# Talking-heads attention before two MLPs: pairs of tiles taken two at a time, or singly

## The chip, the cores and the metric

The kernel runs on one core of a Trainium2 chip. The metric is the time of one execution on the device in microseconds; where several executions were timed it is their median.

Words used below: TensorE does the matmuls, VectorE (DVE in the profile), ScalarE (ACT) and GpSimd (POOL) the elementwise work, and SyncE (SP) issues most DMAs. Each engine works through its own instructions in order and waits for the others by semaphores. A matmul writes into a bank of PSUM, of which there are eight, and another engine copies the result out. In the profile PE is TensorE's matmuls and PEld its weight loads.

## What is computed

Four batches, 12 heads, 448 positions, head dimension 64, all in f32. The heads are mixed before and after the softmax:

```
scores = scale * q @ k^T                       # per head
scores = einsum('bhij,hg->bgij', scores, w_pre)
attn   = softmax(scores, axis=-1)
attn   = einsum('bhij,hg->bgij', attn, w_post)
x      = attn @ v                              # then reshaped to (1792, 768)
x      = square(relu(x @ w_in)) @ w_out        # first MLP, 768 -> 2048 -> 768
h      = x @ w2_in
out    = (h * clip(h + 3, 0, 6) / 6) @ w2_out  # second MLP
```

## The kernel before

**Stages.** The batches are taken in two groups of two. Each group has an attention stage (class `Attention`, line 150) and then an MLP stage (`Mlps` for the first group, line 627; `Blocks` for the second, line 896). The program is one list of instructions in an order written out by hand: every engine gets its instructions in the order in which the Python code calls them.

**Tiles and pairs.** The 448 rows of a batch are cut into tiles of 10 query rows, with all 12 heads side by side on the partitions. Eleven or twelve tiles are a chunk; a group has eight chunks, 90 tiles, and 45 pairs of tiles. A pair is the unit of the work, and *slot* m is the turn of pair m's postmix.

**What happens to a chunk and a pair.**

- `score` (206) is a *visit*: the products of q and k for two heads of one chunk, into two banks. ScalarE copies the one bank (line 209), VectorE the other (211), into the chunk's scores `s`. A chunk takes six visits.
- `fetch` (221) has SP issue two DMAs (230) that bring a pair's rows of `s` into tiles `t`, so that heads lie on the partitions. It is called five slots ahead (`FETCH`).
- `premix` (234): TensorE mixes the heads (242), into two banks.
- `top` (245): VectorE takes each row's maximum (257). `soft` (259): ScalarE takes the exponential and its sum (266). `invert` (270): VectorE adds 1e-9 and inverts (274, 275). `scale` (278): GpSimd multiplies the postmix weights by the inverse, into `w2s` (286).
- `postmix` (290): TensorE mixes the heads again, with the result transposed (299); it is 32 f32 products, which the trace shows as 64 matmuls, each with its own weight load. `keep` (304): ScalarE (318) and VectorE (320) copy its two banks into the chunk's `a`.
- `values` (323): once a chunk's `a` is complete, TensorE multiplies it by V (333; the trace shows 96 matmuls), and VectorE copies the result into `xr` (343).

**Banks.** The pool `ps` (111) has four tags of two banks each. Premixes take `by` and `bm` in turn. Visits, products with V and postmixes take `bs` and `bo`, alternately where the tag comes from `in_turn` (202). A user of a bank waits until the copies of the bank's last user are done.

**The order.** `plan` (388) sets which visits, products with V and loads fall into which slot. `run` (556) goes through the slots. Most of them go in rounds of two, by `two_slots` (493). TensorE's order in a round of slots m and m+1 is: premix m+2, a visit "V", premix m+3, a visit "W", a finished chunk's products with V if there are any, postmix m, postmix m+1, a visit "C". Around these the other engines get, in order: exponentials of m+1 (if still to do) ahead of the first premix; maxima of m+2 on both sides of visit V; exponentials of m+2 behind the second premix; maxima of m+3; exponentials of m+3 ahead of the products with V, or ahead of postmix m+1; inverse and scale of m+2 and copies of m behind postmix m; the same of m+3 and m+1 behind postmix m+1. `rounds` (428) and `places` (432) say where a visit goes. The first slot of the first group and the first three of the second (`PAIRED`, 26) are single, by `slot` (446), and there all visits use the tag `bs`. The slots of negative m, ahead of the first postmix, go through `slot` as well.

**Beside the slots.** In the second group `beside` (1027) is called once for every slot, after the round: it has SP load and store, and GpSimd compute (617), sums of weights for the last MLP stage. `early` (657) converts the first MLP's first unit, called ahead of some products with V. After the last slot `closing` (581) does the last chunk's products with V, into a bank of `bm` and one of `by`.

## Time and profile before

| | |
|---|---|
| Median of 3 runs | 1267.08 us (1262.11 to 1267.51) |
| The profiled execution's own time | 1264.64 us |
| Its span, first to last instruction | 1262.8 us |
| Mean granted clock of TensorE | 0.992 |
| Busy: TensorE / VectorE / ScalarE / GpSimd | 1212.4 / 912.1 / 655.6 / 259.5 us |

The profile is of one execution; its times count from the first instruction. The first attention stage runs from some 16 to 199 us, the first group's MLPs to 667, the second attention stage to 857, and the last MLPs to the end. "Busy" of TensorE is from start to end of its matmuls, which overlap one another, so the time that a group of matmuls takes is read from the starts of two groups that follow each other. In a row of the timeline the bracket at the end tells how long the engine sat idle before the row and what ended it; "issue" stands where nothing that the profile shows was waited for. [...]

### The profile page before, as it was taken

To read this page: it belongs to the slowest core of one execution; us is meant where nothing else is said; L and a number is where in the kernel's file an instruction comes from. 1 tells how busy PE (TensorE), PEld (TensorE's weight loads), DVE (VectorE), ACT (ScalarE), POOL (GpSimd) and SP (SyncE) were. 2 spreads that over 40 slices of the span, in tenths; PEclk is the share of its full clock that TensorE was granted. 3 is DMA by queue.
4 is the path that set the end of the run, shared out by engine and by line. 5 is a ranking of instruction groups with operands and counts; after the bars stand their busy time and mean duration, and the time that the engine had idled before them with its cause. 6 is when DMAs were issued, how large, how long until landed. Compare 5 with 4: busy or idle time off the path is not lost.

```text
span 1262.8 us, 32217 instructions
## 1 busy us (share of the span) xinstructions
PE 1212.4 (96%) x13108; PEld 1058.1 (84%) x13108; DVE 912.1 (72%) x1561; ACT 655.6 (52%) x1268; POOL 259.5 (21%) x349
## 2 busy tenths in 40 slices
PE   8889989999999999999998898979999999999998
PEld 4666778999999999998886666768999999999998
DVE  5666877777665688775556576766977996899885
ACT  5555664545232355532326465657678555456642
POOL 2111133444000033310101343450001220001422
PEclk9999999999999999999999999989999999999999
DMA  6635445766976667677774787757976766685442
GB/s 208 201 118 187 143 147 147 229 190 207 297 220 211 187 203 224 195 235 234 246 267 163 215 271 233 245 198 246 297 247 208 253 200 217 204 285 174 136 135 91
DMA packets 131636, 262.44 MB, mean 208 GB/s; under 512 B 13728, under 2 KB 100384, under 8 KB 131488
## 3 DMA queue, kind: packets, MB, share of 16 engines
q1 hardware_dynamic: 128032, 254.87, 63.2%
q10 hardware_dynamic: 3456, 5.51, 1.2%
q8 instruction: 103, 1.69, 0.6%
q14 instruction: 45, 0.37, 0.1%
HBM read 151.80 MB, written 69.99 MB: 176 GB/s over the span
## 4 chain that ended last, share of the span: by engine, by line
PE 89%; DMA 3%; issue 3%; ACT 3%; DVE 2%; SPq 1%; ACTq 0%; POOL 0%; DVEq 0%; POOLq 0%
PE ps_h L763 18%; PE ps_a L780 18%; PE ps_y L1179 16%; PE ps_w L1079 15%; PE ps_v L333 6%; PE ps_o L299 5%; PE ps_s L199 5%; PE ps_m L242 4%; ACT p L266 2%; DMA t<-s 1%; DVE mx L257 1%; SPq L230 1%; ACT s L209 1%; DVE s L211 0%; DMA first<-in_dram 0%
## 5 line engine op out<-in xcount | busy, mean ns | idle before, releaser
L299 PEld LDWEIGHTS ps_o<-w2s,p 64*64 64x64 f32 x5760 | 102.9, 135 | 49.8 <-issue 41.2
L299 PE MATMUL ps_o<-w2s,p 64*64 64x60 f32 x5760 | 108.6, 220 | 33.0 <-issue 29.4
L780 PE MATMUL ps_a<-gh,wh 128*128 128x448 f32 x384 | 140.2, 365 | 0.0
L780 PE MATMUL ps_a<-gh,wl 128*128 128x448 f32 x384 | 138.4, 360 | 0.0
L722 DVE TENSOR_TENSOR wl<-arena,wh 128x768 fp32r<-128x768 f32 x63 | 61.8, 981 | 102.0 <-ACT wh L721 99.9
L1168 POOL TENSOR_TENSOR o<-gi,o 128x448 fp32r<-128x448 f32 x28 | 57.4, 2052 | 339.4 <-ACT o L1163 232.6
L266 ACT ACTIVATE p<-ps_m,mx 128x448 f32<-128x448 f32 x180 | 112.5, 633 | 23.3 <-DVE mx L257 20.4
L286 POOL TENSOR_SCALAR w2s<-w2f,rz 128x60 f32<-128x60 f32 x180 | 54.6, 317 | 306.2 <-DVE rz L275 215.9
L721 ACT ACTIVATE wh<-arena 128x768 fp32r<-128x768 f32 x63 | 52.8, 839 | 122.8 <-PE ps_a L780 113.8
L257 DVE TENSOR_REDUCE mx<-ps_m 128x1 f32<-128x448 f32 x180 | 104.0, 615 | 11.5 <-PE ps_m L242 10.5
L242 PE MATMUL ps_m<-t,w1f 64*64 64x448 f32 (+1 forms) x720 | 105.2, 566 | 5.1 <-DMA pr<-keep 2.2
L1179 PE MATMUL ps_y<-o,wx 128*128 128x448 f32 x504 | 105.3, 362 | 0.0
L199 PE MATMUL ps_s<-k,q 64*64 64x448 f32 x672 | 99.3, 567 | 4.0 <-ACT s L209 2.6
L1179 PEld LDWEIGHTS ps_y<-o,wx 128*128 128x128 f32 x504 | 94.5, 187 | 6.3
L1179 PE MATMUL ps_y<-o,wh 128*128 128x448 f32 x336 | 99.3, 363 | 0.0
L318 ACT ACTIVATE a<-ps_o 128x480 f32<-128x480 f32 (+1 forms) x98 | 57.2, 595 | 79.3 <-PE ps_o L299 78.5
L756 POOL TENSOR_TENSOR gl<-g,gh 128x448 fp32r<-128x448 f32 x40 | 53.3, 1333 | 203.9 <-ACT gh L755 159.9
L780 PE MATMUL ps_a<-gl,wh 128*128 128x448 f32 x240 | 87.0, 362 | 0.0
L333 PEld LDWEIGHTS ps_v<-a,v 128*64 128x64 f32 x1536 | 75.8, 140 | 12.1 <-issue 6.6
L209 ACT ACTIVATE s<-ps_s 128x448 f32<-128x448 f32 x87 | 47.3, 543 | 69.8 <-PE ps_s L199 65.1
L333 PE MATMUL ps_v<-a,v 128*64 128x110 f32 (+1 forms) x1536 | 79.2, 264 | 1.0 <-DVE a L320 0.9
L780 PEld LDWEIGHTS ps_a<-gh,wh 128*128 128x128 f32 x384 | 72.1, 188 | 9.5 <-issue 4.9
(117 smaller groups left out, 2898.6 us busy)
## 6 DMA issues: line engine op xcount, KB each, us to landing
arena<-in_dram SPq DMA_DIRECT2D x63, 768.0 KB
t<-s SPq DMA_DIRECT2D x176, 210.0 KB
keep<-arena SPq DMA_DIRECT2D x63, 384.0 KB
pr<-keep SPq DMA_DIRECT2D x88, 192.0 KB
wr<-sums_in SPq DMA_DIRECT2D x64, 192.0 KB
wr<-sums_out SPq DMA_DIRECT2D x64, 192.0 KB
low<-wl SPq DMA_DIRECT2D x28, 384.0 KB
wr<-keep SPq DMA_DIRECT2D x48, 192.0 KB
```

The source lines that it names most:

```text
L199: nc.tensor.matmul(out[e][to:to + half_p, :S], lhsT=q[own, to:to + half_p], rhs=keys[own], start=True, stop=True)
L209: nc.scalar.activation(self.s(c)[:, 2 * k, :], out[0][:, :S], AF.Copy)
L242: nc.tensor.matmul(out[a][to:to + half_p, :S], lhsT=w1f[own], rhs=t[own], start=True, stop=True)
L257: nc.vector.reduce_max(mx[:, a:a + 1], out[a][:, :S], axis=AX.X, negate=True)
L266: nc.scalar.activation(pt, o[:, :S], AF.Exp, bias=mx[:, a:a + 1], accum_out=z[:, a:a + 1])
L299: nc.tensor.matmul(out[r][to:to + KB, at:at + G * RI2], lhsT=pt[own, keys:keys + KB], rhs=w2s[own], start=True, stop=True)
L333: nc.tensor.matmul(xo[e * D:(e + 1) * D, k * n:(k + 1) * n], lhsT=self.v[:, q, g, :], rhs=self.aa[c][:, q, g, :n], start=(q == 0), stop=(q ...
L722: nc.vector.tensor_tensor(out=wl, in0=self.wr(n), in1=f(wh), op=ALU.subtract)
L763: nc.tensor.matmul(hp[:, :S], lhsT=lw[:, c * P:(c + 1) * P], rhs=rw[:, c, cols], start=(c == 0 and k == 0), stop=(c == KC - 1 and k == 2))
L780: nc.tensor.matmul(acc[d, e][:, :S], lhsT=lw[:, wc], rhs=rw[fc, e], start=(fc == 0 and k == 0), stop=(fc == NF - 1 and k == 2))
L1079: nc.tensor.matmul(to[:, :S], lhsT=lw[:, wc], rhs=rw, start=(d == 0 and j == 0), stop=(d == DB - 1 and j == 2))
L1179: nc.tensor.matmul(self.acc[d][:, :S], lhsT=lw[:, wc], rhs=rw, start=(u == 0 and q == 0 and j == 0), stop=(u == NU // 2 - 1 and q == UF - ...
```

## The change

Rounds of two slots are gone: every slot from 0 on goes through the new `slot`, which takes one pair. Its order is: fetches; exponentials of pair m+1; premix and both maxima of m+2; a visit "A"; inverse and scale of m+1; products with V if there are any; postmix m; copies of m; a visit "C"; loads of V. The six visits of a chunk are spread over the five slots of its window by the new `places`: one "C" in the first slot, one "A" in each of the others, and one more "C" in the third. All visits, postmixes and products with V in these slots take their banks from `in_turn`, and so do the closing products. The slots of negative m go through `before`, which keeps their order. In the second group's first two slots the six visits of its second chunk stand as "A", "A", "C".

```diff
--- before.py
+++ after.py
@@ -23,7 +23,6 @@
 RAW = 2
 EARLY = 3
 EARLY_AT = 23
-PAIRED = (1, 3)
 IDLE = 2
 GROUP = 2
 PAIRS = 3
@@ -161,7 +160,7 @@
             self.swap = [exchanged(tiles_of(S, NB), i) for i in range(len(self.tiles))]
             self.n = -(-len(self.tiles) // 2)
             self.live, self.ss, self.aa, self.ap, self.xr = {}, {}, {}, None, None
-            self.ks, self.n_raw, self.raw, self.at, self.late, self.turn, self.place = None, 0, None, {}, False, 1, {}
+            self.ks, self.n_raw, self.raw, self.at, self.turn, self.place = None, 0, None, {}, 1, {}
             if gi == 0:
                 self.first_opening()
             self.plan()
@@ -403,12 +402,9 @@
                     for k in range(EARLY, nk):
                         put(top - nk + 1 + k, self.score, c, k)
                     continue
-                if c == 1:
-                    when = [2 * k // nk for k in range(nk)]
-                else:
-                    places = self.places(last[c - 2] - FETCH + 1, top)[-nk:]
-                    when = [slot for slot, _ in places]
-                    self.place.update({(c, k): place for k, (_, place) in enumerate(places)})
+                places = self.places(0 if c == 1 else last[c - 2] - FETCH + 1, top, nk)
+                when = [slot for slot, _ in places]
+                self.place.update({(c, k): place for k, (_, place) in enumerate(places)})
                 for j in range(2):
                     put(when[j * KP] - 4, self.fetch_q, c, j)
                 for k in range(nk):
@@ -425,38 +421,30 @@
             for v in range(NV):
                 put(1 + 3 * v, self.fetch_v, self.batches[0], v)
 
-        def rounds(self, m):
-            m -= PAIRED[self.gi > 0]
-            return None if m < 0 else m % 2
-
-        def places(self, low, top):
-
-            out = []
-            for m in range(low, top + 1):
-                at = self.rounds(m)
-                if at is None:
-                    out += [(m, "A")] * (2 if m == low + 1 else m > low)
-                    continue
-                if at == 0 or m > low:
-                    out.append((m, "VW"[at]))
-                if at == 1:
-                    out.append((m, "C"))
-            return out
-
-        def slot(self, m):
+        def places(self, low, top, count):
+
+            if top < low:
+                return [(2 * k // count, "AAC"[k % (count // 2)]) for k in range(count)]
+            at = [(low, "C")] + [(m, "A") for m in range(low + 1, top + 1)]
+            more = [(m, "C") for m in range(low + 2, top + 1)]
+            return sorted(at + more[:count - len(at)], key=lambda x: (x[0], x[1]))
+
+        def before(self, m):
+
             work = self.at.get(m, [])
 
             def on(fn, k, *args):
                 if 0 <= k < self.n:
                     fn(k, *args)
 
-            def do(name, which=slice(None)):
-                for fn, args in [w for w in work if w[0].__name__ == name][which]:
-                    fn(*args)
+            def do(*names):
+                for name in names:
+                    for fn, args in work:
+                        if fn.__name__ == name:
+                            fn(*args)
             for k in self.fetches.get(m, ()):
                 self.fetch(k)
-            for name in ("fetch_k", "fetch_q", "fetch_v"):
-                do(name)
+            do("fetch_k", "fetch_q", "fetch_v")
             on(self.soft, m + 1)
             if m == -1 and self.gi == 0:
                 self.invert(0)
@@ -464,94 +452,49 @@
                 self.scale(0, 1)
             on(self.premix, m + 2)
             on(self.top, m + 2)
-            visits = [w for w in work if w[0].__name__ == "score"]
-            places = {0: "", 1: "B" if self.late else "A", 2: "BC" if self.late else "AC"}.get(
-                len(visits), "AB" + "C" * len(visits))
-            self.late = "C" in places
-
-            def visit(place):
-                for at, (fn, args) in zip(places, visits):
-                    if at == place:
-                        fn(*args)
-
-            visit("A")
-            if m >= 0 or self.gi > 0:
+            do("score")
+            if self.gi > 0:
                 on(self.invert, m + 1)
-            if 0 <= m < self.n:
-                self.postmix(m)
-            visit("B")
-            if m >= 0 or self.gi > 0:
                 on(self.scale, m + 1, 0)
                 on(self.scale, m + 1, 1)
-            for fn, args in work:
-                if fn.__name__ == "values":
-                    fn(*args, "by" if m % 2 else "bm")
-            if 0 <= m < self.n:
-                self.keep(m)
-            visit("C")
-
-        def two_slots(self, m, early):
-
-            first, second = ([w for w in self.at.get(k, ())] for k in (m, m + 1))
+
+        def slot(self, m, early):
+
+            work = self.at.get(m, [])
 
             def on(fn, k, *args):
                 if 0 <= k < self.n:
                     fn(k, *args)
 
-            def do(name, work):
+            def do(*names):
+                for name in names:
+                    for fn, args in work:
+                        if fn.__name__ == name:
+                            fn(*args)
+
+            def visit(place):
                 for fn, args in work:
-                    if fn.__name__ == name:
-                        fn(*args)
-            visits = [w for w in first + second if w[0].__name__ == "score"]
-
-            def visit(place):
-                for fn, args in visits:
-                    if self.place[args] == place:
+                    if fn.__name__ == "score" and self.place[args] == place:
                         fn(*args, self.in_turn())
             for k in self.fetches.get(m, ()):
                 self.fetch(k)
-            for name in ("fetch_k", "fetch_q"):
-                do(name, first)
-            opens = ("m", m + 1) in self.live
-            if opens:
-                self.soft(m + 1)
+            do("fetch_k", "fetch_q")
+            on(self.soft, m + 1)
             on(self.premix, m + 2)
-            on(self.top, m + 2, False)
-            visit("V")
-            on(self.top_of, m + 2, 1)
-            if opens:
-                self.invert(m + 1)
-                self.scale(m + 1, 0)
-                self.scale(m + 1, 1)
-            for k in self.fetches.get(m + 1, ()):
-                self.fetch(k)
-            for name in ("fetch_k", "fetch_q"):
-                do(name, second)
-            on(self.premix, m + 3)
-            on(self.soft, m + 2)
-            on(self.top, m + 3, False)
-            visit("W")
-            on(self.top_of, m + 3, 1)
-            for fn, args in first + second:
+            on(self.top, m + 2)
+            visit("A")
+            on(self.invert, m + 1)
+            on(self.scale, m + 1, 0)
+            on(self.scale, m + 1, 1)
+            for fn, args in work:
                 if fn.__name__ == "values":
-                    on(self.soft, m + 3)
                     if early:
                         early.pop(0)()
                     fn(*args, self.in_turn())
             self.postmix(m, self.in_turn())
-            on(self.invert, m + 2)
-            on(self.scale, m + 2, 0)
-            on(self.scale, m + 2, 1)
             self.keep(m)
-            if ("m", m + 3) in self.live:
-                self.soft(m + 3)
-            self.postmix(m + 1, self.in_turn())
-            on(self.invert, m + 3)
-            on(self.scale, m + 3, 0)
-            on(self.scale, m + 3, 1)
-            self.keep(m + 1)
             visit("C")
-            do("fetch_v", first + second)
+            do("fetch_v")
 
         def run(self, ap, behind, beside=None, early=None):
 
@@ -561,11 +504,8 @@
                 for step in self.ahead():
                     step()
             for m in range(self.n + 1):
-                two = self.rounds(m) == 0 and m + 1 < self.n
-                if two:
-                    self.two_slots(m, early if m >= EARLY_AT else None)
-                elif m < self.n and m < PAIRED[self.gi > 0] or m == self.n - 1 and ("w", 2 * m) in self.live:
-                    self.slot(m)
+                if m < self.n:
+                    self.slot(m, early if m >= EARLY_AT else None)
                 if beside:
                     beside(ap, m)
                 for step in behind.get(m - self.n, ()):
@@ -576,12 +516,12 @@
 
         def ahead(self):
 
-            return [lambda m=m: self.slot(m) for m in range(-FETCH, 0)]
+            return [lambda m=m: self.before(m) for m in range(-FETCH, 0)]
 
         def closing(self):
 
             c = len(self.chunks) - 1
-            return [lambda v=v: self.values(c, [v], ("bm", "by")[v % 2]) for v in range(NV)]
+            return [lambda v=v: self.values(c, [v], self.in_turn()) for v in range(NV)]
 
 
     kept, low_kept, sums = {}, {}, {}
```

## Rows read from the trace of the kernel before

**Rows 1.** The page: busy us, share of the span, instructions.

```profile
PE 1212.4 (96%) x13108; PEld 1058.1 (84%) x13108; DVE 912.1 (72%) x1561; ACT 655.6 (52%) x1268; POOL 259.5 (21%) x349
```

**Rows 2.** Busy time by stretch: us, busy (count) per engine, PEclk, DMA share, GB/s.

```profile
26.80:198.80 172.00, 154.11 (x4130) 116.97 (x4130) 118.11 (x279) 102.87 (x260) 32.82 (x91) 0.97 0.48 154
...
667.20:857.20 190.00, 164.85 (x4339) 124.25 (x4339) 124.77 (x289) 109.31 (x277) 69.36 (x130) 0.97 0.67 219
...
83.00:89.00 6.00, 6.00 (x123) 4.14 (x117) 4.07 (x8) 3.11 (x8) 0.00 (x0) 0.72 0.09 32
```

**Rows 3.** Timeline of TensorE, first stage: start, us, engine, line, operation, tiles, count.

```profile
92.45 4.74 PE L333 MATMUL ps_v<-a,v 128*64 128x110 f32 x96
97.12 2.09 PE L299 MATMUL ps_o<-w2s,p 64*64 64x60 f32 x128
99.03 0.95 PE L242 MATMUL ps_m<-t,w1f 64*64 64x448 f32 x8
99.79 0.95 PE L199 MATMUL ps_s<-k,q 64*64 64x448 f32 x8
...
102.04 2.43 PE L299 MATMUL ps_o<-w2s,p 64*64 64x60 f32 x128
...
108.03 0.21 PE L299 MATMUL ps_o<-w2s,p 64*64 64x60 f32 x1
```

**Rows 4.** Waits of the whole span: us in total, times, longest.

```profile
PE ps_o L299 <- issue: 29.4, 19, 4.8
```

**Rows 5.** DMA queues, 27 to 199 us: packets, MB, share of 16 engines.

```profile
q8 instruction: 33, 0.54, 1.4%
```

**Rows 6.** Timeline of TensorE around a stop.

```profile
119.46 2.01 PE L299 MATMUL ps_o<-w2s,p 64*64 64x60 f32 x121
123.50 0.28 PE L299 MATMUL ps_o<-w2s,p 64*64 64x60 f32 x4 [2.03 <-issue]
```

**Rows 7.** Timeline of TensorE after another stop.

```profile
81.81 0.50 PE L299 MATMUL ps_o<-w2s,p 64*64 64x60 f32 x17 [2.56 <-issue]
...
82.86 1.70 PE L242 MATMUL ps_m<-t,w1f 64*64 64x448 f32 x8
84.13 1.92 PE L199 MATMUL ps_s<-k,q 64*64 64x448 f32 x8
85.62 1.46 PE L242 MATMUL ps_m<-t,w1f 64*64 64x448 f32 x8
```

**Rows 8.** Timeline of ScalarE: copies of a postmix and of a visit.

```profile
98.33 0.64 ACT L318 ACTIVATE a<-ps_o 128x480 f32<-128x480 f32 x1 [2.92 <-PE ps_o L299]
...
100.78 0.55 ACT L209 ACTIVATE s<-ps_s 128x448 f32<-128x448 f32 x1 [0.83 <-PE ps_s L199]
```

**Rows 9.** Timeline of VectorE in a plain round.

```profile
107.74 1.14 DVE L257 TENSOR_REDUCE mx<-ps_m 128x1 f32<-128x448 f32 x2
108.80 0.61 DVE L211 COPY s<-ps_s 128x448 f32<-128x448 f32 x1
109.33 0.61 DVE L257 TENSOR_REDUCE mx<-ps_m 128x1 f32<-128x448 f32 x1
...
110.21 0.64 DVE L320 COPY a<-ps_o 128x480 f32<-128x480 f32 x1
```

**Rows 10.** Timeline of ScalarE: an exponential.

```profile
110.11 0.62 ACT L266 ACTIVATE p<-ps_m,mx 128x448 f32<-128x448 f32 x1
```

**Rows 11.** Timeline of TensorE in the second stage's single slots.

```profile
670.67 0.98 PE L199 MATMUL ps_s<-k,q 64*64 64x448 f32 x8 [0.67 <-ACT s L209]
672.29 1.10 PE L199 MATMUL ps_s<-k,q 64*64 64x448 f32 x8 [0.65 <-ACT s L209]
```

**Rows 12.** Line 230's instructions on SP: ns min/median/max, first and last start.

```profile
L230 SPq DMA_DIRECT2D t<-s x180: 701/777/1452, 12.0 to 826.7; - x180
```

**Rows 13.** Groups by line: busy us, mean ns, idle before.

```profile
L617 POOL TENSOR_TENSOR pr<-pr 128x384 f32<-128x384 f32 x20 | 20.9, 1046 | 0.8
```

**Rows 14.** Timeline of TensorE at the second stage's closing products.

```profile
847.84 6.62 PE L333 MATMUL ps_v<-a,v 128*64 128x118 f32 x96 [0.89 <-DVE a L320]
```

## The prediction

> **What bounds the kernel now.** I read the page first. TensorE is busy for 96% of the span and no other engine for over 72% [rows 1], so time can come only from where TensorE stops or runs slowly. The busy time by stretch shows where: the two attention stretches, 172.0 and 190.0 us, are the loosely packed ones, with TensorE busy for 154.1 and 164.9 us at a mean granted clock of 0.97 [rows 2]. The change touches these alone.
>
> Next the timeline of TensorE, for the price of each group: what counts is the distance from one start to the next. A premix takes 0.75 us (99.03 to 99.79), a double postmix 1.91 (97.12 to 99.03), so a single one 0.95; a chunk's products with V 4.67 (92.45 to 97.12) [rows 3]. A visit of scores has as many matmuls of the same shape as a premix: 0.75. The first stretch needs 45 postmixes, 43 premixes, 36 visits, 8 products with V and 2.0 us of the MLP's first matmuls: 42.8 + 32.3 + 27.0 + 37.4 + 2.0 = 141.4 us. The second has 42 visits and no MLP matmuls: 143.9. So 30.6 + 46.1 = 76.7 us are lost, and three things lose them.
>
> First, stops that the waits put down to "issue": 29.4 us in 19 stops inside postmixes, up to 4.8 us [rows 4]. I read them as instruction loads. In the first stretch the DMA queues show 33 of them with 0.54 MB [rows 5], 16.4 KB each; its 8,260 matmuls and weight loads [rows 2] make 250 instructions a load, 125 pairs of weight load and matmul. A double postmix is 128 pairs in 1.9 us: it uses up a whole load. A double postmix comes to its end 4.04 us after it began, 2.03 of them a stop [rows 6].
>
> Second, the clock. [...] A mean of 0.97 costs 3% of 172 and 190 us, 10.9 us.
>
> Third, the remaining 36 us: waits for other engines and DMAs, and the stretches' ends. A plain round (two pairs, three visits, no V) should take 1.91 + 2 x 0.75 + 3 x 0.75 = 5.66 us; from 102.04 to 108.03 it takes 6.0 [rows 3]. The 0.34 us between is the second postmix: it takes the two banks that the visit just before the first postmix filled, and those are still being copied out. By the plan of visits 11 rounds of each group have such a visit, 8 of them without V.
>
> **The change, part by part.**
>
> *The second postmix's bank wait.* In the new order a pair of banks comes back two uses later, with a premix and mostly a visit between. 16 x 0.34 = 5.5 us go.
>
> *What the new order waits for instead.* Count a plain slot with one visit from the start of its postmix. TensorE: next premix at 0.95, visit at 1.70, next postmix at 2.45. The copies of a postmix start 1.21 us after it (98.33 against 97.12), those of a visit 0.99 after it (100.78 against 99.79) [rows 3, 8]. VectorE spaces its work 1.06 for two maxima, 0.53 for a copy of scores, 0.88 less 0.53 = 0.35 for the inverse [rows 9], and about 0.55 for a postmix copy: 2.5 us a slot, where TensorE has 2.45. ScalarE takes 0.6 for each of two exponentials [rows 10] and about 0.5 for each of two copies: 2.2. So the postmix's banks are free at 1.2 + 0.2 (VectorE running late) + 0.55 = 1.95, 0.5 before the next postmix. The scale of w2s follows an inverse that VectorE does ahead of that copy, early enough. The exponentials now stand behind the postmix's copy on ScalarE and end at 1.2 + 0.55 + 1.2 = 2.95; the premix that wants their banks comes at 3.4. Every lead is about 0.5 us, and VectorE has nothing over. The new wait per plain slot is therefore between 0 (the leads hold) and 0.5 (a lead is lost; a visit that does wait for its copy loses 0.65 [rows 11]). I take 0.1, VectorE's 0.05 and as much again for hand-overs, near the end that the count gives: 74 slots without V, +7.4 us, range 0 to +37.
>
> *Issue stops.* The number of instructions stays. 125 pairs of the new order hold at most one whole postmix, most of a second, and a premix and a visit between them: about 0.95 + 0.7 + 1.5 = 3.2 us instead of 1.9. With a load ready some 4.04 us after the one before began to be used, the worst ordinary stop falls from 2.1 to 0.8 us. But the mean rate is the same, so short stops appear where there were none, above all in slots 34 to 44, which have no visit. I take 29.4 down to about 20: -9, between 0 and -20.
>
> [...]
>
> *The clock.* It fell after a stop of over 2 us [rows 7], and those become rarer. -4 of the 10.9, between 0 and -8.
>
> *Slots 0 to 2 of the second group.* They are single slots already, with all visits in one pair of banks, and four visits lose 0.64 to 0.67 us each (two of them are shown [rows 11]). With banks in turn: -2.6.
>
> *The visits' new places.* There are as many as before, over five slots instead of about four. A chunk's last visit still comes ahead of the fetch of tiles that needs it, and between that fetch and the premix stand three slots and one product with V, some 12 us. Nothing.
>
> *Queues.* SP issues the two fetches of t ahead of the rest of a slot, at 0.78 us each [rows 12]. The side sums' loads and stores of a slot now come between the fetches of that slot and of the next, where they stood after both. SP then works about 2.2 us in a plain slot of 2.45 in the second group, with the products with V as reserve: nothing, at worst a few late premixes of 1 to 2 us. On POOL one side sum of 1.05 us [rows 13] comes between the scales of two pairs; the scale has about 1 us to spare before its postmix: nothing, at worst part of the 0.5 above.
>
> *Products with V.* They stay in front of a postmix, but only one postmix follows, and ScalarE no longer has a second pair's exponentials to do under them. What hides those now is the next slots' own matmuls, with the leads counted above; if that cover is gone, the exponentials are late first and the premix next.
>
> *Closing products with V.* They leave the premix's banks for those of the last postmixes. They wait 0.89 us for the last postmix's copy already [rows 14], which they need as data; the same copy frees the bank. Nothing.
>
> **Sum**: -5.5 + 7.4 - 9 - 4 - 2.6 = -13.7 us against the profiled execution's 1264.64 (span 1262.8), which is 2.4 below the median of the runs: 1250.9, or **1253** where the median counts.
>
> **Rivals.**
>
> *Slower: lost leads.* The chain of postmix, copy, and the same banks two uses later sits on VectorE, which is as full as TensorE. Without the 7.4 the sum is -21.1; a wait of over 0.29 us in each of 74 slots undoes it, and 0.5 gives +37 - 21.1 = +15.9, **1283**. For it: 2.5 against 2.45, and single slots that wait [rows 11]. Against: those reuse a bank at once, and here a whole use lies between. Chance 0.13.
>
> *Slower: the clock.* [...] Chance 0.07. [...]
>
> *No change: loads set the pace.* If loads come every 4.04 us whatever the order, slots of 72 to 80 pairs take 2.3 to 2.6 us for them, the freed bank waits fill with stops, and only slots 0 to 2 and a little besides stay gained: -5, **1262**. For: the 4.04 us [rows 6]. Against: the 33 loads of the first stretch are 5.2 us apart on average, so most are hidden. Chance 0.15.
>
> *Faster than forecast.* No new wait, stops and clock towards their good ends: -5.5 - 15 - 6 - 2.6 = -29, **1238**. Chance 0.15.
>
> **How the numbers follow.** The forecast has 0.50, by itself 1243 to 1263. A measurement of this kernel can tell half a per cent, 6.3 us, from no change, so the forecast is a gain except for 0.03 of its 0.50. Faster: 0.47 + 0.15 = 0.62; same: 0.15 + 0.03 = 0.18; slower: 0.13 + 0.07 = 0.20. The range goes from 1234 to 1284: it takes in the lost leads at 0.5 us, and leaves out the clock's case and the tails.
>
> **What would show it.** Right: postmixes of 64 pairs, none waiting for a copy; plain slots of about 2.55 us; fewer stops over 2 us inside postmixes and more below 1; a granted clock above 0.97 in both attention stretches, each some 7 us shorter, and everything else as before. Wrong: plain slots over 2.8 us, with postmix or premix waiting for VectorE or ScalarE (lost leads); premixes 1.5 us apart (the clock); 29 us of issue again (loads); or a gain in the first stretch alone, which would point to the queues that only the second one loads.

## The result, and the profile after

The changed kernel took 1246.31 us (the median of 4 runs, 1243.82 to 1251.17), the kernel before 1264.59 in the same session: 0.9861 of it, interval 0.9818 to 0.9904. A second set of runs of both gave 0.9912 (0.9883 to 0.9942; 6 and 17 runs). So it is faster by some 1%, with both medians inside the forecast's range. The profiled execution took 1246.20 us, with a span of 1244.4: 18.4 us less than the one before.

First the page's busy times, to lay beside [rows 1].

```profile
PE 1207.0 (97%) x13108; PEld 1058.9 (85%) x13108; DVE 910.7 (73%) x1561; ACT 650.3 (52%) x1268; POOL 257.8 (21%) x349
```

The same instructions, nearly the same busy time: TensorE lost 5.4 busy us and the span 18.4, so most of the gain is idle time. The busy time by stretch says where, with columns as in [rows 2] (the two attention stages whole, then the surroundings of two stops, then the 6 us that had a clock of 0.72 before):

```profile
21.00:186.80 165.80, 156.38 (x4283) 119.26 (x4282) 123.45 (x292) 105.13 (x274) 34.79 (x96) 0.99 0.52 170
655.90:837.20 181.30, 160.92 (x4330) 124.20 (x4329) 121.88 (x285) 105.51 (x275) 68.17 (x130) 0.97 0.71 227
44.00:55.00 11.00, 6.83 (x105) 6.20 (x98) 2.96 (x7) 2.21 (x6) 0.60 (x2) 0.84 0.78 204
684.00:696.00 12.00, 7.71 (x104) 6.95 (x96) 2.96 (x7) 2.21 (x6) 1.65 (x4) 0.72 0.83 229
83.00:89.00 6.00, 6.00 (x161) 3.49 (x160) 5.36 (x14) 5.08 (x16) 1.67 (x6) 1.00 0.24 87
```

Stage 1 counted from its first postmix, stage 2 from the premix ahead of its first postmix, both to the first matmul behind the last chunk's products with V: stage 1 went from 178.5 to 165.8 us (-12.7) and stage 2 from 187.9 to 181.3 (-6.6); everything else changed by 0.9 us together. Stage 1's granted clock, a share of the full one, rose to 0.99; stage 2's stayed at 0.97.

The waits say which idle time went and which came (us in total, times, longest):

```profile
PEld ps_o L298 <- POOL w2s L285: 20.9, 34, 1.9
...
ACT s L208 <- DMA t<-s: 11.9, 3, 5.4
...
PE ps_o L298 <- issue: 9.0, 10, 2.0
PE ps_v L332 <- ACT s L208: 8.5, 2, 4.3
PE ps_o L298 <- POOL w2s L285: 6.3, 11, 1.4
PE ps_m L241 <- DMA t<-s: 3.0, 4, 1.5
```

Stops at issue inside postmixes fell from 29.4 us [rows 4] to 9.0. Two waits are new: products with V that wait for a copy of scores, 8.5 us in only two stops, and postmixes that wait for their scaled weights w2s, 6.3 us in eleven. TensorE's idle times over 0.1 us in the two stages, summed from its starts and ends, say the same: put to issue, 31.6 us before and 9.0 after; put to anything else, 11.6 and 20.6.

A plain stretch of TensorE in stage 1, to lay beside [rows 3] (start, us, what, count):

```profile
96.73 1.11 PE L298 MATMUL ps_o<-w2s,p 64*64 64x60 f32 x64
97.66 0.99 PE L241 MATMUL ps_m<-t,w1f 64*64 64x448 f32 x8
98.42 0.98 PE L198 MATMUL ps_s<-k,q 64*64 64x448 f32 x8
99.17 1.16 PE L298 MATMUL ps_o<-w2s,p 64*64 64x60 f32 x64
100.21 1.20 PE L198 MATMUL ps_s<-k,q 64*64 64x448 f32 x8
101.01 1.15 PE L241 MATMUL ps_m<-t,w1f 64*64 64x448 f32 x8
101.76 1.15 PE L198 MATMUL ps_s<-k,q 64*64 64x448 f32 x8
102.52 1.21 PE L298 MATMUL ps_o<-w2s,p 64*64 64x60 f32 x58
```

A slot with one visit takes 2.44 us from postmix to postmix, which is the 2.45 counted for its matmuls alone; with two visits 3.35 (3.20 counted). No postmix waits for a bank here.

Now the new stop, TensorE around slot 6 of stage 1, and ScalarE's copy that released it:

```profile
43.41 1.08 PE L198 MATMUL ps_s<-k,q 64*64 64x448 f32 x8
48.66 6.40 PE L332 MATMUL ps_v<-a,v 128*64 128x110 f32 x96 [4.17 <-ACT s L208]
54.99 1.16 PE L298 MATMUL ps_o<-w2s,p 64*64 64x60 f32 x64
```

```profile
48.06 0.54 ACT L208 ACTIVATE s<-ps_s 128x448 f32<-128x448 f32 x1 [5.18 <-DMA t<-s]
```

`places` puts the first visit of chunk c into the first slot of its window, `(low, "C")`. There are two score buffers and chunks alternate, so its copy overwrites the buffer of chunk c-2. The fetch of t for that chunk's last pair was issued only one slot before and still reads it. The copy waits 5.18 us for the fetch, the visit's bank stays full, and the products with V, which take that bank next, stand 4.17 us. Then they need 6.33 us from start to start instead of the 4.67 of [rows 3], at a granted clock of 0.84 in the stretch 44 to 55: 1.00 from 44 to 48, 0.50 from 49 to 52. Stage 2 has the same stop, 4.29 us, with 0.72 granted in the stretch 684 to 696: 1.00 from 684 to 687, 0.50 from 688 to 694. Its row:

```profile
689.01 7.17 PE L332 MATMUL ps_v<-a,v 128*64 128x110 f32 x96 [4.29 <-ACT s L208]
```

In the kernel before, chunk 3's first visit came one slot later, as the first visit of the round of slots 7 and 8 and still ahead of the products with V. ScalarE's copy of it waited for TensorE alone:

```profile
46.52 1.80 PE L199 MATMUL ps_s<-k,q 64*64 64x448 f32 x8
...
50.12 4.74 PE L333 MATMUL ps_v<-a,v 128*64 128x110 f32 x96
```

```profile
48.36 0.54 ACT L209 ACTIVATE s<-ps_s 128x448 f32<-128x448 f32 x1 [1.36 <-PE ps_s L199]
```

Last, the end of stage 1, in slots without visits:

```profile
171.55 1.11 PE L298 MATMUL ps_o<-w2s,p 64*64 64x60 f32 x64
172.75 1.58 PE L241 MATMUL ps_m<-t,w1f 64*64 64x448 f32 x8
174.65 1.16 PE L298 MATMUL ps_o<-w2s,p 64*64 64x60 f32 x64 [0.31 <-POOL w2s L285]
176.84 1.16 PE L298 MATMUL ps_o<-w2s,p 64*64 64x60 f32 x64 [1.03 <-POOL w2s L285]
178.71 1.16 PE L298 MATMUL ps_o<-w2s,p 64*64 64x60 f32 x64 [0.72 <-POOL w2s L285]
```

The last three postmixes wait for the scale of their pair: there are no visits to fill the time, and behind pair 42 no premixes either. A little earlier, in slots 36 to 38, it is ScalarE that has no time left. Besides two exponentials and a postmix's copy each of these slots has a conversion of the first MLP's input (line 671), which the prediction's count of a slot did not have. The stretch, with columns as in [rows 2] (ScalarE's busy time is the fourth, 6.81 of 6.87 us), and one such conversion:

```profile
155.62:162.49 6.87, 6.83 (x220) 3.95 (x213) 6.10 (x17) 6.81 (x20) 3.77 (x8) 1.00 0.58 217
```

```profile
159.67 0.56 ACT L671 ACTIVATE xh<-xr 128x448 fp32r<-128x448 f32 x1
```

These slots take 2.19 to 2.35 us each, where TensorE's two groups need 1.70. From the start of postmix 33 to that of postmix 44 the stages take 33.7 and 35.6 us, 33.2 and 35.2 before: stops at issue went, waits for w2s came. Most of stage 1's gain lies ahead of them (slots 0 to 33: 135.6 to 124.0 us).

### The profile page after: what moved, and what is told of

Its sections match the earlier page's. It is cut to its first block, busy times and chain, and to the rows that moved or that the text cites. A ratio compares the mean times of both kernels' runs of the same rounds, so it can differ in the third digit from the quotient of the medians.

```text
span 1244.4 us, 32289 instructions
## 1 busy us (share of the span) xinstructions
PE 1207.0 (97%) x13108; PEld 1058.9 (85%) x13108; DVE 910.7 (73%) x1561; ACT 650.3 (52%) x1268; POOL 257.8 (21%) x349
## 4 chain that ended last, share of the span: by engine, by line
PE 90%; DMA 3%; DVE 3%; issue 2%; ACT 1%; SPq 0%; POOL 0%; ACTq 0%; POOLq 0%; DVEq 0%
PE ps_a L720 18%; PE ps_h L703 17%; PE ps_w L1019 16%; PE ps_y L1119 16%; PE ps_v L332 7%; PE ps_o L298 6%; PE ps_m L241 4%; PE ps_s L198 4%; DMA t<-s 2%; DVE mx L256 1%; ACT p L265 1%; DMA low<-wl 1%; DVE s L210 1%; DMA first<-in_dram 0%; DVE a L319 0%
## 5 line engine op out<-in xcount | busy, mean ns | idle before, releaser
L298 PEld LDWEIGHTS ps_o<-w2s,p 64*64 64x64 f32 x5760 | 109.5, 134 | 51.2 <-issue 22.4
L298 PE MATMUL ps_o<-w2s,p 64*64 64x60 f32 x5760 | 113.8, 220 | 17.6 <-issue 9.0
L332 PEld LDWEIGHTS ps_v<-a,v 128*64 128x64 f32 x1536 | 79.5, 145 | 19.8 <-ACT s L208 10.0
L332 PE MATMUL ps_v<-a,v 128*64 128x110 f32 (+1 forms) x1536 | 82.9, 271 | 9.3 <-ACT s L208 8.5
L198 PE MATMUL ps_s<-k,q 64*64 64x448 f32 x672 | 88.8, 542 | 0.0
L1019 PE MATMUL ps_w<-b_x,wx 128*128 128x448 f32 x360 | 76.6, 362 | 0.0
```

The lines of the kernel that those rows point to most:

```text
L198: nc.tensor.matmul(out[e][to:to + half_p, :S], lhsT=q[own, to:to + half_p], rhs=keys[own], start=True, stop=True)
L298: nc.tensor.matmul(out[r][to:to + KB, at:at + G * RI2], lhsT=pt[own, keys:keys + KB], rhs=w2s[own], start=True, stop=True)
L332: nc.tensor.matmul(xo[e * D:(e + 1) * D, k * n:(k + 1) * n], lhsT=self.v[:, q, g, :], rhs=self.aa[c][:, q, g, :n], start=(q == 0), stop=(q ...
L1019: nc.tensor.matmul(to[:, :S], lhsT=lw[:, wc], rhs=rw, start=(d == 0 and j == 0), stop=(d == DB - 1 and j == 2))
```

## The experiments

This table is worked out from the starts and ends of TensorE's groups in each trace: stage length in us, idle time over 0.1 us put to issue and to all else (both stages together). "Ratio" is to the kernel before in the same session; rows without one are single runs. A stage ends and begins as above.

| kernel | stage 1 | stage 2 | issue | else | median us | ratio |
|---|---|---|---|---|---|---|
| before | 178.5 | 187.9 | 31.6 | 11.6 | 1264.6 | 1 |
| after | 165.8 | 181.3 | 9.0 | 20.6 | 1246.3 | 0.9861 |
| e8_after_again | 164.8 | 181.2 | 10.1 | 19.1 | 1249.7 | 0.9912 |
| e6_wide_postmix_before | 198.5 | 209.0 | 0.0 | 4.6 | 1305.7 | 1.0372 |
| e7_wide_postmix_after | 201.3 | 208.7 | 0.0 | 6.5 | 1312.6 | 1.0413 |
| e14_half_load_later | 179.6 | 194.5 | 30.7 | 12.2 | 1273.9 | |
| e13_visit_between | 168.8 | 188.7 | 16.2 | 16.8 | 1256.0 | 0.9962 |
| e9_postmix_by_two | 171.0 | 189.0 | 13.7 | 17.1 | 1264.3 | 1.0037 |
| e1_window_late | 165.1 | 178.3 | 9.2 | 16.6 | 1243.2 | 0.9873 |
| e11_v_loads_early | 160.2 | 184.4 | 12.0 | 17.2 | 1245.8 | |
| e12_late_window_v_early | 161.3 | 178.4 | 11.8 | 11.1 | 1244.9 | 0.9892 |
| e4_inverse_first | 164.9 | 190.1 | 13.8 | 17.8 | 1250.9 | 0.9924 |
| e10_late_window_soft_early | 164.2 | 178.8 | 12.7 | 15.3 | 1246.6 | 0.9893 |
| e15_old_banks | 163.4 | 180.5 | 7.0 | 20.4 | 1243.2 | |

### Are the stops instruction loads?

**Fewer, wider products**, in the kernel before and in the changed one: in the postmix two blocks of 64 keys go into one product where both lie in one bank, so the trace has 80 matmuls for two pairs, 48 of them wide, instead of 128.

```diff
+ wide = 2 if q < NK - 1 else 1
+ if q % 2 and q < NK: continue
- out[r][to:to + KB, ...], lhsT=pt[own, keys:keys + KB], ...
+ out[r][to:to + wide * KB, ...], lhsT=pt[own, keys:keys + wide * KB], ...
```

> The kernel before, with the postmix's products 128 keys wide where two blocks of 64 lie side by side: 20 products instead of 32 a pair, so a double postmix is 80 pairs of weight load and matmul instead of 128, less than the 125 of one instruction load. Same result, same order of everything. Theory (the issue stops are instruction loads that a double postmix uses up faster than they come): issue in postmixes falls from 29.4 us to under 8, no stop over 2 us, ratio 0.975 to 0.985, and less if the wide products also run faster. Rival (the stops belong to postmixes as such, whatever their number of instructions): 20 us or more of issue stay, ratio 0.99 to 1.00.

> The changed kernel with the same wide products. Theory (loads): issue in postmixes falls from 9.0 us to under 3; with the wait for the scores' buffer still there, ratio 0.975 to 0.982. Rival (what is left of issue is not loads): 9 us stay, ratio 0.984 to 0.988.

Both were slower: 1305.72 us, 1.0372 (1.0317 to 1.0426), and 1312.64, 1.0413 (1.0368 to 1.0459). The timeline of TensorE in the first and the DMA queues of its stretch 27 to 210 say why (start, us, what, count; packets, MB, share):

```profile
100.45 4.40 PE L302 MATMUL ps_o<-w2s,p 64*128 64x60 f32 x80
104.67 0.94 PE L242 MATMUL ps_m<-t,w1f 64*64 64x448 f32 x8
```

```profile
q8 instruction: 24, 0.39, 0.9%
```

The 80 matmuls of a double postmix (the row is named after its first shape) take 4.22 us, where 128 narrow ones took 1.91. No stop at issue inside postmixes is left, but this is no clean test: the loads fell from 33 in 172 us [rows 5] to 24 in 183 us, and the postmixes also use them up at less than a third of the rate. The wide products also cost TensorE time of their own (see the last section). It fits the reading as loads and does not prove it; as a cure it costs more than it saves.

**The borders moved.** In the kernel before, 32 small products on zeros are put ahead of everything. The trace shows them as 64 matmuls with 64 weight loads. They shift every later instruction of TensorE against the loads' borders by these 128, half a load, and add no work to another engine.

```diff
+ for k in range(32):
+     nc.tensor.matmul(warm_bank[:64, :60], lhsT=idle[:64, :64], rhs=idle[:64, :60], ...)
```

> The kernel before, with 32 small products on zeros put ahead of everything, while the first loads are on their way: 64 pairs of weight load and matmul, half an instruction load, so that every border between loads falls 64 pairs earlier in the program; nothing else moves. Theory (a stop comes where a border between loads falls late in a double postmix): of the 13 stops over 0.8 us inside postmixes of the kernel before (pairs 4, 5, 14, 24, 40, 42, 44 of the first stage, 8, 9, 16, 26, 42, 44 of the second) at most 2 are still at the same product, and others appear where a border now falls late; their sum stays between 15 and 35 us, and each lies within 2 us of an instruction load. Rival (stops belong to a slot, by what its DMAs or copies do): at least 8 stay at their pairs.

The sum stays, in the table and in the waits of this kernel:

```profile
PE ps_o L299 <- issue: 24.7, 12, 4.2
```

The places go. Counted as pair and product, the stops over 0.8 us inside postmixes of the kernel before and of this one were (stage 1, then stage 2):

```
before  4@26 5@57 14@46 24@57 40@46 42@27 44@26 | 8@18 9@41 16@33 26@46 42@57 44@56
e14     6@57 8@52 20@38 41@27 43@26             | 10@41 12@46 22@26 32@39 41@58 43@57
```

None of the 13 stayed where it was, and those at the stages' ends came one postmix (64 products) earlier, to within one product: 42@27 to 41@27, 44@26 to 43@26, 42@57 to 41@58, 44@56 to 43@57. A stop that belonged to data would have stayed with its pair. The count of instructions says more: the stops of stage 1 before come after 941, 1195, 2965, 4987, 8021, 8271 and 8525 of TensorE's weight loads and matmuls, in steps of 254, 7 x 253, 8 x 253, 12 x 253, 250 and 254, where [rows 5] gave 250 to a load. The stops at 41@27 and 43@26 of this run come after 8271 and 8525 again. Each of the 13 stops before also has a packet of the instruction queue in it or up to 1.8 us ahead of it. So the stops stand at borders of loads, whichever pair is there: they are loads. Single ones last up to 4.2 us.

This run took 1273.87 us, 9.2 more than the profiled execution before, of which 6.6 in stage 2; with one run, whether the new places of the stops cost that is open.

### Is it the order?

**One visit between.** In the kernel before, the visit "C" moves from behind a double postmix to between its two halves.

```diff
  self.keep(m)
+ visit("C")
  ...
  self.keep(m + 1)
- visit("C")
```

> The kernel before, with visit C of a round between its two postmixes instead of behind them (about 11 rounds of a group have one); all else as before. Theory (two postmixes in a row use up a load): stops over 0.8 us go from rounds with a visit C and stay in the others (from pair 33 on none has one), issue in postmixes 10 to 20 us instead of 29, ratio 0.990 to 0.997; the second postmix waits about 0.2 us for the first one's copy in each of these rounds. Rival (a visit between makes no difference): issue 25 us or more, ratio 0.998 to 1.004.

1255.98 us, 0.9962 (0.9944 to 0.998): a small part of the gain. Stops inside postmixes fell to 16.2 us, from 29.4:

```profile
PE ps_o L299 <- issue: 16.2, 11, 4.2
```

Stage 1 got 9.7 us shorter, three quarters of what the whole change gave it, and stage 2 no shorter. The stops that stayed were not all in rounds without such a visit: three of them (pairs 13/14 and 26 of stage 2) have one. So a visit between lowers the stops without excluding them, and why it helped only stage 1 is open.

**Postmixes by twos again.** In the changed kernel even slots do no postmix and odd ones do two, each followed by its copies; the rest of the new order stays.

```diff
- self.postmix(m, self.in_turn())
- self.keep(m)
+ for k in [m] if m == self.n - 1 and m % 2 == 0 else [m - 1, m] if m % 2 else []:
+     self.postmix(k, self.in_turn())
+     self.keep(k)
```

> The changed kernel, with one thing put back: an even slot does no postmix, and the odd slot behind it does both in a row, with their copies between. Visits, banks in turn, single premixes stay as changed. Theory (the change gains by not doing two postmixes in a row, since two use up a whole instruction load in 1.9 us): issue in postmixes goes back to 22 to 32 us from 9, stops over 2 us come back, ratio 0.994 to 1.003. Rival (the gain is in banks and in the visits' places): issue stays under 14 us, ratio 0.984 to 0.989.

1264.25 us, 1.0037 (1.0011 to 1.0064): the gain is gone, and a little more. But not through the stops that I had named, as its waits show:

```profile
PEld ps_m L241 <- ACT p L265: 28.1, 45, 1.8
...
PE ps_o L298 <- issue: 6.7, 9, 2.2
```

Stops inside postmixes sum to less than in the changed kernel (the table's 13.7 has 7.0 in premixes and products with V). Instead the weight loads of premixes wait for exponentials; the copies of two postmixes stand ahead of them on ScalarE. In the changed kernel and in the kernel before, which also did two at once, that wait was small:

```profile
PEld ps_m L241 <- ACT p L265: 6.8, 12, 1.7
```

```profile
PEld ps_m L242 <- ACT p L266: 8.1, 13, 2.3
```

The time came out as my theory had it and its reason did not. So this run is no way back to the kernel before: it shows that the new order of exponentials and copies needs single postmixes, and not that they alone carry the gain. Besides, pair 0's postmix moves to slot 1, and the first postmix starts at 24.70 us instead of 21.01. Two postmixes in a row are also not enough for stops at issue; that the new waits gave the loads time here is likely and not shown.

### What the new stop at slot 6 costs

**A later window.** The first visit of a chunk comes one slot later, so that the fetch has read the buffer.

```diff
- at = [(low, "C")] + [(m, "A") for m in range(low + 1, top + 1)]
- more = [(m, "C") for m in range(low + 2, top + 1)]
+ at = [(m, "A") for m in range(low + 1, top + 1)]
+ more = [(m, "C") for m in range(low + 1, top + 1)]
```

> The changed kernel, but a chunk's window opens one slot later: no visit in its first slot; the second and third slots hold an A and a C each. Theory (the visit's copy overwrites scores that a fetch of t is still reading, and TensorE then stands 4.2 and 4.3 us before the products with V of slot 7): both waits go or fall under 1 us, the products behind them take 4.7 instead of 6.4 us, each attention stage 4 to 6 us shorter, ratio to the kernel before 0.977 to 0.981. Rival (the stop is a DMA that is late anyway and shows up at the next premix): the waits move to another line, ratio stays at 0.986.

1243.17 us, 0.9873 (0.9835 to 0.9911): not to be told from the changed kernel. Both stops are gone and stage 1 is still 165.1 us. TensorE's timeline in stage 1 has this instead:

```profile
57.65 1.20 PE L298 MATMUL ps_o<-w2s,p 64*64 64x60 f32 x64
62.20 1.09 PE L241 MATMUL ps_m<-t,w1f 64*64 64x448 f32 x8 [3.35 <-DMA k<-in_dram]
```

The premix waits for a DMA; the row names the load of K that landed then, the premix itself reads t. I read this as the wait having moved on to a later transfer, with the stop at slot 6 the place where late transfers were felt first. Stage 2, where no such wait followed, got 3 us shorter.

**V earlier.** Stage 1's loads of V are issued in slots -4 and -1 instead of 1 and 4; stage 2 is as it was.

```diff
- put(1 + 3 * v, self.fetch_v, self.batches[0], v)
+ put((1 if self.gi else -4) + 3 * v, self.fetch_v, self.batches[0], v)
```

> The changed kernel, with the two loads of V of the first stage in slots -4 and -1 instead of 1 and 4. Theory (the 4.2 us before slot 7's products with V are fetches of t that land late because the DMA queues are full there, and the visit's copy may not overwrite what they read): the stop in the first stage falls under 2 us, the one in the second stage, whose loads stay, stays near 4. Rival (the stop is set by SP's order or by the scores' buffer whatever the load): 4 us in both.

One run, 1245.75 us. The row that was 6.40 us long and stood behind 4.17 is now this; what is left of waiting comes earlier and is shorter:

```profile
31.80 1.16 PE L298 MATMUL ps_o<-w2s,p 64*64 64x60 f32 x64 [2.28 <-ACT s L208]
...
46.10 4.74 PE L332 MATMUL ps_v<-a,v 128*64 128x110 f32 x96
```

Stage 1 takes 160.2 us, 5.6 less, of which 1.8 goes back because its first postmix starts later. Stage 2, untouched, keeps its stop (4.9 us). So moving the V loads took the stop away in the stage where they were moved and left it in the other. That they made the fetch late fits their place in SP's order: in the changed kernel SP issues a load of V at 35.78 us and two fetches of t right behind it, at 36.85 and 37.76. It is one run, and it does not show how.

**Both together**: the later window and the early V.

```diff
+ at = [(m, "A") for m in range(low + 1, top + 1)]
+ more = [(m, "C") for m in range(low + 1, top + 1)]
+ put((1 if self.gi else -4) + 3 * v, self.fetch_v, self.batches[0], v)
```

> The changed kernel with the later window and, in the first stage, the earlier loads of V. Theory (what is left early in each stage is fetches of t that land late): the first stage under 164 us from its first postmix, the second near 178, ratio 0.978 to 0.987, 4 to 8 us under the changed kernel. Rival (each of the two only moves the wait to the next premix): stages of 165 and 181 us, ratio 0.987 to 0.992.

1244.9 us, 0.9892 (0.987 to 0.9914). The stages are 161.3 and 178.4, together 7.4 below the changed kernel's, but the first postmix comes 3.3 us later (24.27), and the median can't be told from the changed kernel's. I found no version that is clearly faster than the changed kernel.

### Who makes w2s late?

**The inverse first.** In the changed kernel invert and scale go ahead of visit "A".

```diff
- visit("A")
  on(self.invert, m + 1)
  on(self.scale, m + 1, 0)
  on(self.scale, m + 1, 1)
+ visit("A")
```

> The changed kernel, with the inverse and scale of a pair ahead of visit A instead of behind it. Theory (the chain exponential, inverse, scale, postmix has lost its lead; 20.9 us of weight loads of postmixes wait for w2s): that wait falls to under 10 us, 2 to 5 us shorter than the changed kernel, ratio 0.982 to 0.985. Rival (the lead is lost on ScalarE, where the exponentials stand behind the postmix's copy, so VectorE's order does not matter): w2s waits stay at about 20 us, ratio 0.986, or VectorE now waits for ScalarE and visits' copies come late: ratio up to 0.990.

1250.86 us, 0.9924 (0.9897 to 0.9952). The waits of the weight loads for w2s fell and those at issue on TensorE rose:

```profile
PE ps_o L298 <- issue: 13.5, 11, 3.8
...
PEld ps_o L298 <- POOL w2s L285: 13.5, 17, 1.5
```

No gain: the time between postmixes was not set by w2s alone. Part of the rival came true: with the inverse ahead of it VectorE's copy of a visit comes late, and weight loads of the next visit wait for it:

```profile
PEld ps_s L198 <- DVE s L210: 6.6, 21, 0.7
```

**Exponentials ahead of the copies**, in slots from 34 on, together with the later window:

```diff
  self.postmix(m, self.in_turn())
+ if m >= 34: on(self.soft, m + 2)
  self.keep(m)
```

> The window that opens a slot later, and in slots 34 to 44, which have no visit, the exponentials of pair m+2 ahead of the copy of postmix m on ScalarE instead of behind it. Theory (there the postmix waits for w2s because the exponentials stand behind that copy): w2s waits of postmixes fall from 19 us to under 10, 2 to 5 us less than with the late window alone, ratio 0.981 to 0.985. Rival (VectorE or GpSimd sets the pace there, or instruction loads do): waits move to VectorE's inverse or to issue, ratio 0.985 to 0.989.

1246.57 us, 0.9893 (0.9865 to 0.992). The waits did not fall, and slots 33 to 44 took 33.1 and 35.7 us:

```profile
PEld ps_o L298 <- POOL w2s L285: 25.0, 30, 2.6
```

So ScalarE's order is not what sets these slots. In slots 37 and 38 of stage 1 its amount of work is: ScalarE (the fourth busy time) has no idle time in this run either:

```profile
156.31:161.02 4.71, 3.91 (x144) 2.36 (x144) 4.14 (x11) 4.71 (x15) 3.44 (x7) 1.00 0.50 186
```

What sets the other slots, and those of stage 2, is open.

### The banks

**Old banks in two places**: slots 0 to 2 of the second group go back to one pair of banks each for visits and postmixes, and the closing products with V to the premix's banks.

```diff
- fn(*args, self.in_turn())
+ fn(*args, "bs" if self.gi and m < 3 else self.in_turn())
- self.postmix(m, self.in_turn())
+ self.postmix(m, "bo" if self.gi and m < 3 else self.in_turn())
- self.values(c, [v], self.in_turn())
+ self.values(c, [v], ("bm", "by")[v % 2])
```

> The changed kernel with two parts put back: in slots 0 to 2 of the second group all visits in one pair of banks, and the closing products with V in the premix's banks. Theory: the three slots take 2 to 3 us longer, with visits waiting 0.6 us for ScalarE's copy; the closing products start after the last postmix's copy as in the changed kernel, within 0.3 us of its 0.89 us wait, and what follows is the same. Rival for the closing: they start up to 0.6 us earlier, because they no longer wait for a bank.

The three slots take 15.55 us instead of 13.1, with visits that wait for a copy again, as in [rows 11]; the closing products wait exactly as long as in the changed kernel and in [rows 14]:

```profile
656.83 0.98 PE L198 MATMUL ps_s<-k,q 64*64 64x448 f32 x8 [1.60 <-ACT s L208]
...
661.94 1.12 PE L198 MATMUL ps_s<-k,q 64*64 64x448 f32 x8 [0.64 <-ACT s L208]
...
665.43 1.10 PE L198 MATMUL ps_s<-k,q 64*64 64x448 f32 x8 [0.64 <-ACT s L208]
...
828.22 5.06 PE L332 MATMUL ps_v<-a,v 128*64 128x118 f32 x96 [0.89 <-DVE a L319]
```

The whole kernel, one run of 1243.20 us, can't be told from the changed kernel.

**The changed kernel again**, with no edit:

> The changed kernel once more, beside the next ones on one chip. Both theories: ratio 0.984 to 0.988 as before; it is the measure for the others.

1249.68 us, 0.9912. Its stages agree with the first profile's within 1 us, and its two long stops behind a copy of scores are there again (8.2 us); of the five stops at issue over 0.8 us in postmixes three are at the same product.

## Why the prediction was right, and where its steps were not

The sign and size held: -13.7 us forecast, -18.4 between the two profiled executions, -18.3 and -8.8 by the medians of the two sets. The terms held less well, and that the sum came so near is in part luck: the stops at issue fell by some 11 us more than their term, and two stops that had no term cost some 12.5 with the slow products behind them.

- *The second postmix's bank wait* (-5.5): right in kind, somewhat small in fact. In the trace before, 12 of the 16 second postmixes behind such a visit come 0.32 to 0.40 us late, some 4.4 us together. Afterwards a plain slot takes its matmuls' 2.44 us, and waits of postmixes for visits' copies sum to 2.1 us. No run undid this alone.
- *What the new order waits for* (+7.4, 0.1 us in each of 74 slots): wrong as to place. The 24 slots with one visit and no V take 2.49 and 2.46 us in the middle (the medians of the two stages), so the leads of 0.5 us hold there and VectorE is not the bound, at 74% busy in stage 1. The 25 slots with a premix and neither visit nor V take 2.28 and 2.62, where TensorE's groups need 1.70: there, as I read it, exponentials, inverse and scale have too little to hide behind, and in stage 1 ScalarE has a conversion besides. Of idle time other than issue, 8.5 us in two stops and 6.3 in eleven waits for w2s came, and some 6 us of other waits went: 9.0 more.
- *Issue stops* (-9, between 0 and -20): undersized; -20.4, just past the good end. The step that failed is "short stops appear where there were none, above all in slots 34 to 44". In those slots issue fell from 5.0 to 0.3 us in stage 1 and from 3.1 to 0.9 in stage 2, and waits for w2s came. The whole of stage 1 keeps 0.5 us of 16.0, stage 2 8.5 of 15.6, with stops of up to 1.96 us where 0.8 was to be the worst ordinary one. That they are loads is now shown by the moved borders. Most loads go by without a long stop: stage 1 before has 7 stops over 0.8 us to some 33 loads.
- *The clock* (-4, between 0 and -8): right in size. From 0.97 to 0.99 in stage 1 is 2% of 166 us, 3.3; nothing in stage 2 (0.97 before and after), where 0.50 was granted from 688 to 694, during the new stop and behind it. The rival of a clock that falls more often did not come: groups of a microsecond alternate and the spacing stays at 0.75, as from 97.66 to 99.17. In the two stretches read here the granted clock went from 1.00 to 0.50 around stops of 4.17 and 4.29 us; in the kernel before it was 0.55 from 82.8 to 85.6, behind the stop of 2.56 us in [rows 7].
- *Slots 0 to 2* (-2.6): right; -2.1 in the profile after, 2.45 given back by the old banks.
- *The visits' new places* (nothing): this is the step that was wrong. I asked whether a chunk's last visit comes ahead of the fetch that needs it, and did not ask whether its first visit comes behind the fetch that still reads the buffer. In the kernel before it came a slot later. The price is 4.17 + 4.29 us of stops and some 1.7 and 2.4 us of products with V at a lower clock (0.50 granted from 49 to 52 and from 688 to 694). As the later window shows, that is not what a cure gives back: in stage 1 the next transfer was late too.
- *The rivals*: lost leads would have shown plain slots over 2.8 us, and loads that set the pace 29 us of issue; neither is there (2 of the 24 plain slots with one visit are over 2.8), though 35 loads in 166 us are no fewer than before.
- *SP's queue* (nothing, at worst late premixes of 1 to 2 us): right for premixes, which wait 3.0 us for t in 4 stops. *Closing products* (nothing): right, 0.89 us in all three kernels.
- "A gain in the first stretch alone would point to the queues that only the second one loads": stage 2 gained half as much. Its DMA share is 0.71 against 0.52, and a visit between the postmixes helped only stage 1. That is a hint, not proof; why stage 2 gains less stays open. So does the split of the gain between loads and order: the sums of idle time put most of it on the stops at issue, and no run takes them out alone.

## What to carry to other kernels

Where many small matmuls follow each other, count them against an instruction load: here some 250 weight loads and matmuls, by 33 loads in the first stage and stops 250 to 254 apart or at multiples of 253. Here a longer group between two dense ones lowered the stops (29.4 to 16.2 us) without excluding them. Test a suspicion by a few idle instructions at the front, which move the borders and leave the other work in its order. When work is moved earlier, check for each buffer it writes who still reads it, not only who reads it next. Count the slots that have least work for the bound engine by themselves: here the others' chain showed there, with 2.28 and 2.62 us a slot where TensorE's groups need 1.70. And before curing the largest new wait, ask what is late behind it: with the 4.17 us stop of stage 1 gone here, a premix waited 3.35 us for another transfer.

## What the runs showed of the hardware

Products of 64*128 were far dearer than I expected: a double postmix with 48 of them and 32 of 64*64 took 4.22 us, against 1.91 for 128 of 64*64, which is 15 ns each. With 15 ns for each of the 32 narrow ones, 0.48 us, some 78 ns are left for each wide one, the changes of shape included: an estimate, some five times a narrow one for twice the keys. The place of an instruction in the program decided whether it stopped: 64 matmuls with their weight loads at the front moved all 13 stops over 0.8 us and nearly left the idle time at issue as it was, 31.6 and 30.7 us. Products with V that followed a stop of 4.17 us took 6.33 us instead of 4.67, at a granted clock of 0.84 in that stretch, and 7.09 (689.01 to 696.10) after one of 4.29 us, at 0.72.
